# Moving the fourth cell of the head, and subtracting its sums on TensorE, in a fused mLSTM and gated MLP kernel

## The chip, the cores and the metric

The kernel runs on one core of one Trainium2 chip. The metric is the device time of one launch in microseconds (us). The engines are named as in the profile: PE is TensorE, with PEld for its loads of stationary operands; DVE is VectorE; ACT is ScalarE; POOL is GpSimd; SP issues most of the DMAs.

## The reference

Two blocks run one after the other. The first is an mLSTM cell over 4 batches, 8 heads, 768 steps and 40 dimensions a head:

```python
for t in range(S):
    m_new = np.maximum(f_gate[:, :, t] + m, i_gate[:, :, t])
    f_stab = np.exp(f_gate[:, :, t] + m - m_new)
    i_stab = np.exp(i_gate[:, :, t] - m_new)
    C = f_stab * C + i_stab * outer(vt, kt)
    n = f_stab * n + i_stab * kt
    y[:, :, t] = sigmoid(o_gate) * (C @ qt) / np.maximum(np.abs(n . qt), 1.0)
```

(The last lines are shortened.) The second takes the result as x, 3072 rows of 320, and computes `h = x @ w_in` (320 x 2048), `g = h * np.cos(h)`, `g @ w_out` (2048 x 320). The weights w_in and w_out come in 64-bit floats, which the kernel turns into 32-bit floats itself.

## The kernel before

The steps are cut into 6 chunks of 128. A cell n is one batch of one chunk: n = 4 * chunk + batch, 24 cells in all. Within a chunk the recurrence is written as products: with a running sum of the forget gates and a running maximum, cell n has a matrix E of decays, one 128x128 block for each of 8 heads. The scores of keys and queries (`scores`) are multiplied by E (`weigh`), and the products of that with the values (`values`) give the cell's output, which `normalize` divides by its denominator and multiplies by the sigmoid of the o gate. `seam` turns the output, so that it can be the input of the second block, and makes the increment of the carried state; `seam_out` and `state` copy both out of PSUM.

The first four cells (chunk 0) are the head of the kernel, `first_cells`. After it comes `first_period`, where the second block of chunk 0 begins beside cell 4 (`B` is 4); from there on both blocks are interleaved to the end. The order of the instructions on each engine is the order of the calls in the program, written by hand: no scheduler moves them. Each engine takes its own instructions in that order and waits where one is not ready, and so does the queue of SP for its DMAs.

For a cell of the head, `maxima_in` makes on PE, in PSUM, the running maxima of all its heads, spread over the partitions, with a wall of 1e30 above the diagonal. It is a product of the identity with `wall` and four products of `of_parts` columns (ones that pick a row) with `M0_parts`, which holds the maxima as the sum of three bf16 parts. `less_sums` subtracts, on DVE and in two halves of 128x512, what `tab` holds for each row, the input gate less the running sum (`a0`, turned); `decay` takes the exponential of the negative on ACT.

The gates of the other five chunks are worked out beside the head, by the 32 rows of batch and head: `gates_sums` and `gates_maxima` are scans on DVE, `gates_less_sums` and `gates_shifts` small steps, and `gates_carry` makes the carried factors and writes them to DRAM as G_d; the maxima go to M_d. `gates_exp` takes exponentials of `a1` less the chunk's last maximum, `gates_turn` turns `a1` and these exponentials by PE transposes of 32x128, and `gates_turn_out` copies both into `tab`.

The weights of the second block come in pieces: `weights_in(0)` issues the DMAs of the first two pieces (4 DMAs of 128 KB each, line 163) and of a low piece (4 of 64 KB, line 217). For each piece, `take_apart` is two steps on ACT (lines 175 and 177), `bound` two and `join` one on DVE (lines 181, 182 and 191), and `round_up` one on POOL (line 196). `warm` issues products of zeros on PE, which nothing reads.

Lines that the text speaks of: 749 and 743 first products of the second block; 757 their rounding on ACT (`near`); 863 the down products; 576 values and 560 scores of the head; 566 `weigh`; 650 to 658 `normalize`; 692 to 701 `seam`; 712 `seam_out`; 1096 `warm`; 325 `gates_turn`; 332 a small product for the carried factors; 328 `gates_turn_out`; 476 `decay` of later cells; 436 loads of E from M_d.

Of the kernel before, what the change touches and what calls it, by code (L numbers as in the profile page):

```python
# [11 lines left out]
FP = mybir.dt.float32  # L12
# [17 lines left out]
def kernel(  # L30
# [20 lines left out]
    nc = tc.nc  # L51
# [36 lines left out]
    M0_parts = small[:, 704:768].bitcast(BF)  # L88
    of_parts = small[:, 768:784].bitcast(BF)
    nc.vector.memset(nil, 0.0)  # L90
    ident = const.tile([128, 128], FP, name="ident")
# [8 lines left out]
    nc.vector.memset(M0_parts, 0.0)  # L100
    nc.vector.memset(of_parts, 0.0)

    nc.gpsimd.memset(wall, 0.0)
# [66 lines left out]

    def take_apart(dst, bits):
        n = dst.shape[1]
        hi, lo = bits[:, 0:n, 1], bits[:, 0:n, 0].bitcast(U32)

        nc.scalar.activation(out=dst, in_=hi.bitcast(FP), func=AF.Abs)

        nc.scalar.activation(out=bits[:, 0:n, 0], in_=lo, func=AF.Copy, scale=2.0 ** -29)
# [62 lines left out]
    nM1 = gates.tile([BH, R], FP, name="nM1")  # L240
    dd = gates.tile([BH, R - 1, BH], FP, name="dd")

    def gates_constants():
# [23 lines left out]
    def maxima_in_parts():  # L267
# [8 lines left out]
        nc.scalar.copy(out=M0_parts[BH:2 * BH], in_=mid)  # L276

    def gates_first_out():
        pg = ps_o.tile([128, 2, BH], FP, name="pg", tag="o")
        for j, src in enumerate((a0, e0)):  # L280
            nc.tensor.transpose(pg[:, j], src, ident[0:BH, 0:BH])
        nc.vector.tensor_copy(out=tab[:, 0, 0:2], in_=pg)
# [3 lines left out]

    eW, eG = shift, keep

# [24 lines left out]

    def gates_exp():
        for c in range(R):
            nc.scalar.activation(out=eW[:, c], in_=a1[:, c], func=AF.Exp, bias=nM1[:, c:c + 1])

# [4 lines left out]

    def gates_turn(pg, j):
        for c in range(R):
            nc.tensor.transpose(pg[:, c, j], (a1, eW)[j][:, c], ident[0:BH, 0:BH])

    def gates_turn_out(pg):
        nc.scalar.copy(out=tab[:, 1:NC, 0:2], in_=pg)

# [139 lines left out]
    def decay(n, heads=range(H)):  # L469
        c, b = divmod(n, B)  # L470
        if n < B:
            nc.scalar.activation(out=Es[n], in_=Es[n], func=AF.Exp, scale=-1.0)
            return
        for h in heads:
            g = b * H + h
            nc.scalar.activation(out=Es[n][:, h], in_=Es[n][:, h], func=AF.Exp, scale=-1.0, bias=tab[:, c, 0, g:g + 1])  # L476
# [167 lines left out]

    def normalize(n):
        c, b = divmod(n, B)
        hs = heads_of[n]
# [4 lines left out]
        nc.vector.reciprocal(out=dn, in_=dn)  # L652
        y = p1.tile([128, 3 * C], FP, name="y", tag="yt")[:, 0:DM]
        t = yo.rearrange("q (h d) -> q h d", h=H)
        nc.vector.tensor_tensor(out=t, in0=sig[c][:, b], in1=hs[:, :, 0:D], op=OP.mult)
        for lo, hi, o in ((0, 32, y[:, 0:KL].rearrange("q (g a d) -> q a g d", g=2, a=HP)),
                          (32, D, y[:, KL:DM].rearrange("q (a g d) -> q a g d", g=2, a=HP))):
            nc.vector.tensor_tensor(out=o, in0=t[:, :, lo:hi].rearrange("q (a g) d -> q a g d", g=2),
                                    in1=dn.rearrange("q (a g) -> q a g", g=2).unsqueeze(3).to_broadcast([128, HP, 2, hi - lo]), op=OP.mult)
# [448 lines left out]
    def first_cells():  # L1108
# [41 lines left out]
        weigh(0)  # L1150
        sigmoid_next()
        sigmoid(0)
        exp_next()
        gates_sums()
        gates_less_sums()
# [5 lines left out]
        less_sums(2)  # L1161
        decay(2)
        values(1)
        normalize(0)
        normalize(1)
        maxima_in(3)
        less_sums(3)
        turn(2)
        turn_out(2, False)
        weigh_k(2)  # L1170
        seam(0)
        seam_out(0)
        scores(2)
        state(0)
        decay(3)
        weigh(2)
        seam(1)
        seam_out(1)
        weigh_k(3)
        gates_maxima()  # L1180
        gates_shifts()
        load_M(B)
        load_blocks(B)
        load(B, "kv")
        outs.append((0, weights_out(0)))
        turn(3)
        turn_out(3, False)
        values(2)
        normalize(2)
        state(1)  # L1190
        gates_carry()
        load_G_of(B)
        load_blocks(B + 1)
        pg = ps_a.tile([128, R, 2, BH], FP, name="pg", tag="a")
        gates_turn(pg, 0)
        scores(3)
        take_apart(*pieces[0])
        seam(2)
        weigh(3)
        bound(pieces[0][0])  # L1200
        seam_out(2)
        gates_exp()
        take_apart(*pieces[1])
        warm(2, psum_o())
        values(3)
        join(*pieces[0])
        round_up(*pieces.pop(0))
        state(2)
        more = weights_in(1)
        pieces.append(next(more))  # L1210
        normalize(3)
        warm(6, psum_o())
        gates_turn(pg, 1)
        bound(pieces[0][0])
# [4 lines left out]
        seam_out(3)  # L1219
        gates_turn_out(pg)  # L1220
        take_apart(*pieces[0])
# [12 lines left out]
        decay(B)  # L1234
        odd_constants()
        odd_values_of(B)
# [418 lines left out]
```

## Time and profile before

| | us |
|---|---|
| median of 3 runs | 504.28 (503.46 to 504.53) |
| the profiled execution | 503.72 |
| its span, from the first to the last instruction | 501.9 |
| PE busy | 495.1 (99%) |
| DVE busy | 420.6 (84%) |
| ACT busy | 332.5 (66%) |
| POOL busy | 300.0 (60%) |

The profile is of one execution, whose own time stands beside its span. A timeline row has the start, the length, the engine, the line, the operation, its output and inputs, the shape and how many instructions are merged; in brackets stands how long the engine had been idle, and what released it. Matmuls are pipelined, so the length of a group on PE reaches over the start of the next; the time from start to start is what a group costs in a full stream. An f32 matmul appears as two instructions, a transpose as one. The granted clock of PE is 1.00 through the whole span.

### The profile page before, as it was taken

How to read it: one execution, taken by the hardware profiler on the slowest of the kernel's cores; microseconds unless marked ns; L12 is line 12 of the kernel's file. 1: busy time of each engine (PE TensorE's matmuls, PEld its weight loads, DVE VectorE, ACT ScalarE, POOL GpSimd, SP SyncE). 2: the span in 40 equal slices, each digit the busy share in tenths (PEclk: the TensorE clock that was granted, in tenths of full speed). 3: DMA queues.
4: the chain of work that ended last, by engine and by line, in shares of the span. 5: the costliest groups of instructions: out<-in, count | busy, mean ns of one | idle time of the engine just before them, and what ended most of it. 6: DMA issues, size and time to landing. Idle time of an engine off the chain costs nothing.

```text
span 501.9 us, 11143 instructions
## 1 busy us (share of the span) xinstructions
PE 495.1 (99%) x4038; PEld 375.4 (75%) x4038; DVE 420.6 (84%) x842; ACT 332.5 (66%) x646; POOL 300.0 (60%) x394
## 2 busy tenths in 40 slices
PE   9999999999999999999999999999999999999997
PEld 6856656565667668887887888788788888787876
DVE  7899998999878878899889889889979866777565
ACT  6799997878564575765877846777847743443541
POOL 8254557666555576787558877657567446434340
PEclk9999999999999999999999999999999999999999
DMA  9989899997366346129446118628113000010001
GB/s 139 182 223 239 213 224 279 233 217 136 114 178 111 101 120 127 50 86 202 132 125 106 48 54 195 168 83 150 43 35 85 1 7 5 2 54 0 2 0 54
DMA packets 100663, 56.74 MB, mean 113 GB/s; under 512 B 63456, under 2 KB 93360, under 8 KB 100608
## 3 DMA queue, kind: packets, MB, share of 16 engines
q1 hardware_dynamic: 97408, 54.43, 46.8%
q10 hardware_dynamic: 2896, 1.23, 1.0%
q8 instruction: 32, 0.52, 0.5%
q0 software_dynamic: 304, 0.36, 0.3%
q14 instruction: 23, 0.19, 0.1%
HBM read 50.66 MB, written 4.10 MB: 109 GB/s over the span
## 4 chain that ended last, share of the span: by engine, by line
PE 85%; ACT 4%; DVE 3%; DMA 2%; SPq 2%; POOL 2%; issue 1%; DVEq 0%; ACTq 0%; POOLq 0%
PE acc L1014 24%; PE pup L817 17%; PE pup L749 9%; PE po L863 6%; PE pup L833 6%; PE late L1014 5%; PE ps L560 4%; PE pup L743 3%; PE vt L595 2%; PE vt L586 2%; PE pu L701 2%; PE ph L576 1%; DMA E<-M_d 1%; DMA vs<-in_v_dram 1%; DVE n L760 1%
## 5 line engine op out<-in xcount | busy, mean ns | idle before, releaser
L757 ACT ACTIVATE n<-pup 128x512 int32<-128x512 f32 x64 | 37.0, 593 | 84.2 <-DVE pup L842 58.4
L765 ACT ACTIVATE n<-n 128x512 f32<-128x512 f32 x96 | 57.7, 626 | 16.5 <-DVE n L760 12.5
L852 POOL TENSOR_TENSOR g<-g,n 128x512 f32<-128x512 f32 x31 | 39.6, 1278 | 47.5 <-ACT n L765 47.4
L749 PE MATMUL pup<-xT,w_in_sb 128*128 128x512 f32 x128 | 58.7, 601 | 0.3 <-ACT xT L712 0.2
L1014 PE MATMUL acc<-w_out_sb,g 128*128 128x160 f32 x320 | 58.7, 303 | 0.0
L760 DVE SCALAR_TENSOR_TENSOR n<-pup,n 128x512 f32<-128x512 f32 x64 | 43.1, 689 | 18.5 <-ACT n L757 15.9
L834 POOL TENSOR_TENSOR blocks<-blocks 128x256 f32<-128x256 f32 x32 | 25.1, 785 | 54.5 <-ACT blocks L826 54.5
L1014 PE MATMUL acc<-T,g 128*128 128x160 f32 x304 | 56.4, 301 | 0.0
L817 PE MATMUL pup<-xT,w_in_sb 128*128 128x256 f32 x192 | 53.5, 385 | 0.2
L476 ACT ACTIVATE E<-E,tab 128x128 f32<-128x128 f32 x160 | 50.1, 389 | 4.3 <-POOL E L462 4.1
L1014 PEld LDWEIGHTS acc<-w_out_sb,g 128*128 128x128 f32 x320 | 49.0, 190 | 4.7 <-issue 2.7
L769 DVE TENSOR_TENSOR g<-pup,n 128x512 f32<-128x512 f32 x64 | 42.7, 687 | 5.7 <-ACT n L765 4.8
L1014 PEld LDWEIGHTS acc<-T,g 128*128 128x128 f32 x304 | 46.5, 190 | 1.1 <-issue 0.4
L749 PEld LDWEIGHTS pup<-xT,w_in_sb 128*128 128x128 f32 x128 | 23.1, 189 | 30.7 <-issue 30.0
L825 ACT COPY blocks<-pup 128x512 f32<-128x512 f32 x32 | 18.6, 582 | 34.2 <-PE pup L817 33.8
L817 PEld LDWEIGHTS pup<-xT,w_in_sb 128*128 128x128 f32 x192 | 33.8, 189 | 9.6 <-ACT blocks L826 4.4
L817 PE MATMUL pup<-x_room,room 128*128 128x256 f32 x128 | 38.5, 382 | 0.0
L542 POOL TENSOR_TENSOR qG<-t,G 128x512 f32<-128x512 f32 x20 | 26.4, 1321 | 16.7 <-DVE t L538 16.7
L1014 PE MATMUL acc<-T,blocks 128*128 128x160 f32 x160 | 36.2, 308 | 0.2 <-POOL blocks L904 0.2
L863 PE MATMUL po<-w_out_sb,g 128*128 128x320 f32 x128 | 36.2, 436 | 0.1
L833 PE MATMUL pup<-xL,w_in_l 64*128 64x512 f32 x128 | 36.1, 641 | 0.0
L566 DVE TENSOR_TENSOR E<-ps,E 128x512 f32<-128x512 f32 x46 | 29.5, 682 | 5.8 <-PE ps L560 5.6
(227 smaller groups left out, 1210.7 us busy)
## 6 DMA issues: line engine op xcount, KB each, us to landing
E<-M_d SPq DMA_DIRECT2D x20, 512.0 KB, 6.0
qr<-in_q_dram SPq DMA_DIRECT2D x72, 80.0 KB, 2.6
kr<-in_k_dram SPq DMA_DIRECT2D x72, 80.0 KB, 2.2
bits<-in_moe_w_out_dram SPq DMA_DIRECT2D x8, 640.0 KB, 6.2
G<-G_d SPq DMA_DIRECT2D x18, 256.0 KB, 5.7
blocks<-in_moe_w_in_dram SPq DMA_DIRECT2D x32, 128.0 KB, 4.6
out_dram<-o_sb SPq DMA_DIRECT2D x23, 160.0 KB, 1.8
o<-in_o_gate_dram SPq DMA_DIRECT2D x40, 80.0 KB, 4.4
```

The costliest lines, as they stand in the source:

```text
L476: nc.scalar.activation(out=Es[n][:, h], in_=Es[n][:, h], func=AF.Exp, scale=-1.0, bias=tab[:, c, 0, g:g + 1])
L566: nc.vector.tensor_tensor(out=w, in0=pss[n][j], in1=w, op=OP.mult)
L749: nc.tensor.matmul(pu.rearrange("p (b t) -> p b t", b=B), w_in_sb[:, i, ts(2 * f2 + e, 128)], xT[c][:, i:NK * B:NK], start=(i == 0 and not ...
L757: nc.scalar.activation(out=self.n[e], in_=self.pu[e], func=AF.Copy, bias=0.25)
L760: nc.vector.scalar_tensor_tensor(out=self.n[e].bitcast(FP), in0=self.pu[e], scalar=0.25, in1=self.n[e], op0=OP.add, op1=OP.subtract)
L765: nc.scalar.activation(out=r, in_=r, func=AF.Sin, scale=TWO_PI_DOWN)
L769: nc.vector.tensor_tensor(out=g, in0=self.pu[e], in1=self.n[e].bitcast(FP), op=OP.mult)
L817: nc.tensor.matmul(bank[:, part].rearrange("p (b t) -> p b t", b=B // 2), w[:, f2], x, start=start, stop=stop, skip_group_check=True)
L833: nc.tensor.matmul(pu, w_in_l[r, f2], xL[c][r].rearrange("p b t -> p (b t)"), start=False, stop=True, skip_group_check=True)
L852: tt(out=self.g, in0=self.g, in1=self.n[e].bitcast(FP), op=OP.mult)
L863: nc.tensor.matmul(po[c][b], gs[c, f][:, ts(b, C)], w_out_sb[:, f], start=(f == 0), stop=(f == NF - 1))
L1014: nc.tensor.matmul(a, lhs, rhs, start=start, stop=stop)
```

## The change

Four things change, all in the head.

Cell 3 gets its exponents on PE alone. `sums_in_parts` splits the negative of `a0` into three bf16 parts (five steps on DVE, one on ACT), and `exponents_in(3)` adds, to the wall and the maxima, one more product a half, of `a0_parts` with columns of `of_parts`. `less_sums(3)` goes, and the exponential of cell 3 reads PSUM, in two instructions. These products stand ahead of `values(1)`.

The exponentials of the later gates are taken after the turn: `gates_exp` and the second `gates_turn` go; `gates_last` makes on DVE a diagonal `dM` of the last maxima, `gates_less_last` adds `a1` turned by the identity and ones times `dM` on PE, 10 products of 32x128 by 32x32, and `gates_turn_out` is a copy and an exponential.

The calls of the head are put in another order. The scan of the maxima stands before `normalize(1)`; cell 3 is turned before cell 1's `seam`; `take_apart` of the first piece is split, its first step before `seam_out(1)`, its second after it; `bound`, `join` and `round_up` of that piece, and `gates_last`, stand before cell 2's `normalize` on DVE, which is itself split around `weigh(3)`; `seam(2)` stands behind `values(3)`. On SP, cell 4's blocks, k and v come before its E. The four memsets of `odd_constants` go from the end of the head to before `gates_less_sums`.

The fillers between the last cells go from 2 and 6 to 2 and 2.

```diff
+    def sums_in_parts():
+        rest, mid = blocks[0:BH, 38], blocks[0:BH, 39].bitcast(BF)[:, 0:C]
+        hi = a0_parts[0:BH]
+        nc.vector.tensor_scalar(out=hi, in0=a0, scalar1=-1.0, scalar2=None, op0=OP.mult)
+        nc.vector.scalar_tensor_tensor(out=rest, in0=a0, scalar=-1.0, in1=hi, op0=OP.mult, op1=OP.subtract)
+        nc.vector.tensor_copy(out=mid, in_=rest)
+        nc.vector.tensor_tensor(out=rest, in0=rest, in1=mid, op=OP.subtract)
+        nc.vector.tensor_copy(out=a0_parts[2 * BH:3 * BH], in_=rest)
+        nc.scalar.copy(out=a0_parts[BH:2 * BH], in_=mid)
+
+    def exponents_in(n):
+        for i in range(2):
+            g = n * H + HP * i
+            wall_in(n, i, psum_o())
+            nc.tensor.matmul(pm[n, i], a0_parts, of_parts[:, g:g + HP].unsqueeze(2).to_broadcast([128, HP, C]),
+                             start=False, stop=False)
+            spread(n, i)
...
-    def gates_exp():
-        for c in range(R):
-            nc.scalar.activation(out=eW[:, c], in_=a1[:, c], func=AF.Exp, bias=nM1[:, c:c + 1])
+    def gates_last():
+        nc.vector.tensor_tensor(out=dM, in0=ident[0:BH, 0:BH].unsqueeze(1).to_broadcast([BH, R, BH]),
+                                in1=nM1.unsqueeze(2).to_broadcast([BH, R, BH]), op=OP.mult)
...
+    def gates_less_last(pw):
+        for c in range(R):
+            nc.tensor.matmul(pw[:, c], a1[:, c], ident[0:BH, 0:BH], start=(c == 0), stop=False)
+            nc.tensor.matmul(pw[:, c], one.to_broadcast([BH, 128]), dM[:, c], start=False, stop=(c == R - 1))
+
+    def gates_turn_out(pg, pw):
+        nc.scalar.copy(out=tab[:, 1:NC, 0], in_=pg)
+        nc.scalar.activation(out=tab[:, 1:NC, 1], in_=pw, func=AF.Exp)
...
+            E = Es[n]
+            for i in range(2):
+                nc.scalar.activation(out=E[:, ts(i, HP)], in_=pm[n, i], func=AF.Exp, scale=-1.0)
...
         decay(2)
+        exponents_in(B - 1)
         values(1)
         normalize(0)
+        gates_maxima()
+        gates_shifts()
         normalize(1)
-        maxima_in(3)
-        less_sums(3)
         turn(2)
         turn_out(2, False)
         weigh_k(2)
+        decay(3)
         seam(0)
+        load_blocks(B)
+        load(B, "kv")
+        load_M(B)
+        outs.append((0, weights_out(0)))
+        scores(2)
         seam_out(0)
-        scores(2)
-        state(0)
-        decay(3)
         weigh(2)
+        turn(3)
+        turn_out(3, False)
+        take_high(*pieces[0])
         seam(1)
         seam_out(1)
         weigh_k(3)
-        gates_maxima()
-        gates_shifts()
-        load_M(B)
-        load_blocks(B)
-        load(B, "kv")
-        outs.append((0, weights_out(0)))
-        turn(3)
-        turn_out(3, False)
-        values(2)
-        normalize(2)
+        take_low(*pieces[0])
+        state(0)
         state(1)
         gates_carry()
         load_G_of(B)
         load_blocks(B + 1)
-        pg = ps_a.tile([128, R, 2, BH], FP, name="pg", tag="a")
-        gates_turn(pg, 0)
-        scores(3)
-        take_apart(*pieces[0])
-        seam(2)
-        weigh(3)
+        values(2)
         bound(pieces[0][0])
-        seam_out(2)
-        gates_exp()
-        take_apart(*pieces[1])
-        warm(2, psum_o())
-        values(3)
         join(*pieces[0])
         round_up(*pieces.pop(0))
-        state(2)
+        scores(3)
+        pgs = ps_a.tile([128, 2, R, BH], FP, name="pg", tag="a")
+        gates_turn(pgs[:, 0])
+        gates_last()
+        gates_less_last(pgs[:, 1])
+        bank = psum_o()
+        warm(2, bank)
+        y = weighted(2)
+        weigh(3)
+        divided(2, y)
+        take_apart(*pieces[0])
+        values(3)
+        warm(2, bank)
         more = weights_in(1)
         pieces.append(next(more))
+        seam(2)
+        seam_out(2)
+        state(2)
         normalize(3)
-        warm(6, psum_o())
-        gates_turn(pg, 1)
         bound(pieces[0][0])
         put_together(*pieces.pop(0))
...
         decay_exponents(B)
         seam(3)
         seam_out(3)
-        gates_turn_out(pg)
+        gates_turn_out(pgs[:, 0], pgs[:, 1])
```

More of the change, by code (lines that the diff above doesn't have):

```diff
@@ L89 @@
     of_parts = small[:, 768:784].bitcast(BF)
+    a0_parts = small[:, 784:848].bitcast(BF)
     nc.vector.memset(nil, 0.0)
@@ L101 @@
     nc.vector.memset(of_parts, 0.0)
+    nc.vector.memset(a0_parts, 0.0)
     nc.gpsimd.memset(wall, 0.0)
@@ L171, in take_apart, with take_high, take_low @@
     def take_apart(dst, bits):
+        take_high(dst, bits)
+        take_low(dst, bits)
+    def take_high(dst, bits):
+        nc.scalar.activation(out=dst, in_=bits[:, 0:dst.shape[1], 1].bitcast(FP), func=AF.Abs)
+    def take_low(dst, bits):
         n = dst.shape[1]
-        hi, lo = bits[:, 0:n, 1], bits[:, 0:n, 0].bitcast(U32)
-        nc.scalar.activation(out=dst, in_=hi.bitcast(FP), func=AF.Abs)
+        lo = bits[:, 0:n, 0].bitcast(U32)
         nc.scalar.activation(out=bits[:, 0:n, 0], in_=lo, func=AF.Copy, scale=2.0 ** -29)
@@ L241 @@
     dd = gates.tile([BH, R - 1, BH], FP, name="dd")
+    dM = gates.tile([BH, R, BH], FP, name="dM")
     def gates_constants():
@@ L285 @@
     flat = [t.rearrange("r c s -> r (c s)") for t in (F1, M1, a1, keep, shift)]
-    eW, eG = shift, keep
+    eG = keep
     def gates_sums():
@@ L321, in gates_diagonal, with gates_turn @@
                                 in1=eG[:, 0:R - 1, last].to_broadcast([BH, R - 1, BH]), op=OP.mult)
-    def gates_turn(pg, j):
+    def gates_turn(pg):
         for c in range(R):
-            nc.tensor.transpose(pg[:, c, j], (a1, eW)[j][:, c], ident[0:BH, 0:BH])
-    def gates_turn_out(pg):
-        nc.scalar.copy(out=tab[:, 1:NC, 0:2], in_=pg)
+            nc.tensor.transpose(pg[:, c], a1[:, c], ident[0:BH, 0:BH])
+    def gates_less_last(pw):
[5 more added lines that the diff above has]
+        nc.scalar.activation(out=tab[:, 1:NC, 1], in_=pw, func=AF.Exp)
     def gates_spread():
@@ L470, in decay @@
         c, b = divmod(n, B)
+        if n < B - 1:
+            nc.scalar.activation(out=Es[n], in_=Es[n], func=AF.Exp, scale=-1.0)
+            return
         if n < B:
-            nc.scalar.activation(out=Es[n], in_=Es[n], func=AF.Exp, scale=-1.0)
+            E = Es[n]
+            for i in range(2):
+                nc.scalar.activation(out=E[:, ts(i, HP)], in_=pm[n, i], func=AF.Exp, scale=-1.0)
             return
@@ L645, in normalize, with weighted @@
     def normalize(n):
+        divided(n, weighted(n))
+    def weighted(n):
         c, b = divmod(n, B)
@@ L652, in normalize, with divided @@
         nc.vector.reciprocal(out=dn, in_=dn)
-        y = p1.tile([128, 3 * C], FP, name="y", tag="yt")[:, 0:DM]
         t = yo.rearrange("q (h d) -> q h d", h=H)
         nc.vector.tensor_tensor(out=t, in0=sig[c][:, b], in1=hs[:, :, 0:D], op=OP.mult)
+        return t, dn
+    def divided(n, of):
+        t, dn = of
+        y = p1.tile([128, 3 * C], FP, name="y", tag="yt")[:, 0:DM]
         for lo, hi, o in ((0, 32, y[:, 0:KL].rearrange("q (g a d) -> q a g d", g=2, a=HP)),
@@ L1151, in first_cells @@
         sigmoid_next()
+        gates_sums()
+        sums_in_parts()
         sigmoid(0)
         exp_next()
-        gates_sums()
+        odd_constants()
         gates_less_sums()
@@ L1234, in first_cells @@
         decay(B)
-        odd_constants()
         odd_values_of(B)
```

## The prediction

> **What bounds the kernel now.** The page's first part comes first: PE is busy for 99% of the span, and the chain that ended last (part 4) is 85% PE. From 55 us on I find PE without gaps that this change could touch, so the change is worth what it moves the start of that stretch. I therefore read the timelines of the first 60 us, engine by engine. TensorE, around the last two cells of the head:
>
> ```profile
> 22.04 1.88 PE L576 MATMUL ph<-vs,E 128*128 128x41 f32 x16
> 23.85 0.49 PE L325 MATMUL pg<-ident,w_out_sb 32*128 32x32 f32 x5
> 24.27 1.16 PE L560 MATMUL ps<-t,t 64*128 64x128 f32 x16
> ...
> 26.95 1.87 PE L576 MATMUL ph<-vs,blocks 128*128 128x41 f32 x16
> 28.65 1.47 PE L1096 MATMUL pm<-room 128*128 128x512 bf16 x6
> 30.05 0.49 PE L325 MATMUL pg<-ident,w_out_sb 32*128 32x32 f32 x5
> 30.54 0.41 PE L692 MATMUL px<-ident,y 128*128 128x128 f32 x2
> ```
>
> The columns are start, length, engine, line, operation. Groups follow start to start: PE looks full, but L1096 is filler, which means waiting. VectorE says for what:
>
> ```profile
> 25.54 1.29 DVE L566 TENSOR_TENSOR blocks<-ps,blocks 128x512 f32<-128x512 f32 x2
> 26.91 0.50 DVE L181 TENSOR_SCALAR w_in_sb<-w_in_sb 128x512 f32<-128x512 f32 x1
> ...
> 28.86 0.17 DVE L650 SCALAR_TENSOR_TENSOR dn<-ph,least 128x8 f32<-128x8 f32 x1 [0.18 <-PE ph L576]
> ```
>
> The chain is: scores of cell 3, end 25.43; their weighing (L566), end 26.83; values of cell 3, 26.95 to 28.65; its normalizing; its turned output at 30.54 (call this the pivot). From the start of cell 3's values to the pivot is 30.54-26.95 = 3.59 us, whatever PE does beside it. Behind the pivot ScalarE carries the path without a gap:
>
> ```profile
> 31.37 0.37 ACT L712 COPY xT<-px 128x256 f32<-128x256 f32 x1
> 31.64 0.43 ACT L328 COPY tab<-pg 128x320 f32<-128x320 f32 x1
> 31.95 0.45 ACT L175 ACTIVATE w_in_l<-blocks 128x256 f32<-128x256 f32 x1
> ...
> 34.82 2.45 ACT L476 ACTIVATE E<-E,tab 128x128 f32<-128x128 f32 x8
> 37.29 1.08 ACT L757 ACTIVATE n<-pup 128x512 int32<-128x512 f32 x2
> ```
>
> From 37.29 to 55.40 the busy time by stage is 17.66 of 18.11 us for ACT and 17.04 for DVE, so a delay of the first rounding (L757) passes through to the end.
>
> **Up to cell 2's values: nothing.** The changed program has the products of cell 3's maxima and sums ahead of cell 1's values. From 13.14 us (maxima of cell 2) on PE, start to start: maxima 0.88; cell 3's exponents, 0.88 like these plus two more 128x512 bf16 products at 0.22, 1.32; values 1.77; turn 0.88; turned output of cell 0 1.02; scores 1.09; turn 0.88; turned output of cell 1 1.02: 8.86, so cell 2's values start at 22.0, against 22.04. What is saved on order (0.2 of waiting for v) is paid by the two products. The five small DVE steps that make the parts cost what the same five cost at L271 to L275, 3.71 to 5.29, 1.58; they lie in a gap of 1.53 before cell 1's weighing: 0 to 0.1. DVE loses the subtraction of cell 3 (2 x 0.64), and ACT gets its exponential as two 128x512 from PSUM instead of one 128x1024: both are off the path here. POOL's four memsets (36.00 to 37.25, 1.25) now stand before the subtraction of the later gates (11.85); it then ends at 14.9, and its reader, the maxima scan, starts at 17.2: hidden; if that cover went, up to 1.25 for the scan. SP issues E's load after the next cell's blocks, k and v, near 28.0 instead of 26.70; with the 4.8 to 6.7 us that such loads took it lands by 34.7 at worst, before its mask (about 35): hidden, narrowly.
>
> **Where it hurts: the first piece of w_in.** ACT's first conversion of that piece now follows the turned copies of cell 3, which end near 21.7, and DVE's bounding and joining of it stand ahead of cell 3's weighing. Has the piece landed? SP's queue:
>
> ```profile
> 17.59 4.42 SPq L163 DMA_DIRECT2D blocks<-in_moe_w_in_dram  x8
> 22.37 2.71 SPq L217 DMA_DIRECT2D blocks<-in_moe_w_in_dram  x4
> ...
> DMA to landing us min/median/max: 4.0/4.1/4.2
> ```
>
> The first piece is the first four of the eight. The fourth is issued at 19.72, so it lands at about 19.72+4.1 = 23.8. Bounds: not before 22.35, when the first L217, which the built program makes wait for the landing of the first of the eight, went out; not after 24.5, when the last L217, which waits for the fourth, had started. Nothing ahead of these issues changes on SP. So ACT stands from 21.7 to 23.8, with cell 1's copies, its states and the carry queued behind it, and DVE, done with cell 2's weighing at 21.95, stands to 23.8+0.66 = 24.46. Then DVE: bound and join 1.77 (26.91 to 28.68 before), 26.2; the new product dM (32x160; L320's 32x128 took 0.27) 0.3, 26.5; the first half of cell 2's normalizing 0.99 (23.96 to 24.95), 27.5; cell 3's weighing 1.29, 28.8, where it ended at 26.83.
>
> **PE between.** Scores of cell 3 end at 24.9 (0.5 earlier: cell 1's output and the first turn of the gates are no longer in between), five transposes 0.42, 25.35. Then come ten new f32 matmuls, each two passes: a 32x128 stationary, 32 columns moving. They wait for dM at 26.5; 18 of 20 passes are left. The nearest rows for one pass:
>
> ```profile
> L576 PEld LDWEIGHTS ph<-vs,E 128*128 128x128 f32 x48 | 5.6, 192 | 0.3 <-DVE E L566 0.3
> L325 PEld LDWEIGHTS pg<-ident,w_out_sb 32*128 32x128 f32 x10 | 0.8, 136 | 0.5 <-ACT w_in_sb L175 0.4
> L332 PEld LDWEIGHTS pd<-dd,one 32*128 32x128 f32 x2 | 0.3, 182 | 0.1
> ```
>
> L325 has the same shape, but is a transpose: 136 ns a load and 0.42/5 = 0.084 from start to start. L332 is a true f32 matmul with 32 rows, and its load of 182 ns is near L576's 192, which runs at 1.71/16 = 0.107 a pass. I take 0.107: 18 x 0.107 = 1.93, 28.45 (with 0.084: 1.51, 28.0). [...] Two fillers 0.44: cell 3's values start at 28.9, against 26.95: **+1.95**. DVE's 28.8 would give nearly the same, so both would have to improve. Behind them the two fillers and cell 2's output fit in the 3.59 (1.70+0.44+1.02 = 3.16); four fillers and five transposes fewer there save nothing, for the normalizing ends last.
>
> **ACT behind the pivot.** One 128x320 copy becomes a 128x160 copy and a 128x160 exponential; the 128x128 forms took 0.25 and 0.30, so about 0.27+0.32 less 0.31 to 0.43: +0.15 to +0.3, taken as **+0.25**. The five 32x128 exponentials that go (1.57) had 0.13 us of waiting behind them, off the path.
>
> **Carry.** It moves from 24.74 to about 26.9 on ACT, so G lands some 2 us later and SP waits about 3 us for it; its readers are delayed by the same 2 us, and their slack stays: nothing.
>
> **Sum.** +1.95+0.25 = +2.2. The profiled execution took 503.72 (span 501.9 and 1.8 around it), which gives 505.9; the three runs' median lies 0.56 above it, which gives 506.5. I take the middle, **506.2**. With the landing at 22.4 the values start at 27.55 (+0.6, +0.85 in all), at 24.5 at 29.6 (+2.65, +2.9); the cheap pass takes up to 0.4 off.
>
> **Rivals.** (1) The piece is there when ACT asks, at 21.7. Then DVE bounds it in its gap, the weighing ends at 26.5, and PE decides alone: 25.35+20 x 0.107+0.44 = 27.9, +1.0 and 0.25: 505.4; at 0.084 a pass 504.9. Against it: the landing rows. For it: only that the order would then fit. It straddles the line of no change. (2) Not slower: the new products overlap, at the 0.0275 a pass of L701's 16 in 0.44 (its stationary has 40 columns), and the piece lands by 21.7. Then DVE's 26.5 decides the values' start, 0.45 before now; with 0.25 paid behind the pivot that is -0.2, 503.8. If the exponential hides, and L181 and L182 on the last piece of w_in (2.25 us at 32.44, while POOL is busy; 0.29 and 0.30 at 73.41) get free of POOL's mask, PE's idle 0.56 before L743 goes too: -1.0, 503.0. It needs passes under 0.05 and a landing before 22.0; no row with 128 columns shows that. (3) Clock: PE stands about 1.1 us for dM and 0.4 before the pivot. The granted clock was 1.00 in all stages, with an idle 0.56 at most in this stretch. If it were halved for the 3 us of work that follow, 1.5 to 3 more: 508. (4) The later G costs: SP's wait of 3 us reaches the second part of w_in, whose first conversion had 2 us of slack: 0 to +1 more, 507.
>
> [...]
>
> **Numbers.** Chances: forecast 0.70, (4) 0.06, (1) 0.14, (2) 0.07, (3) 0.03. A measurement here tells 0.2% (1.0 us) from no change. The forecast's case falls under +1.0 only with an early landing and the cheap pass (0.06 of its 0.70), (1) is half within, and of (2) I give 0.04 to its better end: slower 0.64+0.06+0.07+0.03 = 0.80, within 0.06+0.07+0.03 = 0.16, faster 0.04. The range 504.2 to 507.8 reaches from below (1) to the late landing with some of (4); (2), (3) and the ends of the others are left out.
>
> **What would show it.** In the changed kernel: ACT idle for about 2 us before its first conversion of w_in, released by a DMA; DVE idle from about 22 to 24.5; dM near 26.3; the ten products with a pass near 0.1; cell 3's values at 28.9, its turned output at 32.5 and the first rounding at 39.5, 2.2 late. Wrong if the conversion starts at 21.7, if the values start before 27.5, or if the roundings are late and the end is not.

## The result and the profile after

| | before | after |
|---|---|---|
| median, us | 504.4 (4 runs, 503.46 to 505.51) | 509.0 (4 runs, 508.88 to 510.38) |
| ratio, 95% interval | | 1.0096 (1.0070 to 1.0123) |
| profiled execution, its span | 503.72, 501.9 | 508.88, 507.0 |
| mean granted clock of PE | 1.0 | 0.993 |

The kernel is slower by 4.6 us, the profiled span by 5.1. The forecast was +2.2 and its range ended at 507.8. PE around the last two cells, for the changed kernel (values are L614 now, scores L598, seam L737 to L746, filler L1141; L475 begins cell 3's exponents; L356 and L357 are the ten products):

```profile
15.84 0.38 PE L475 MATMUL pm<-room 128*128 128x512 bf16 x1 [1.02 <-DVE E L604]
...
23.88 1.98 PE L614 MATMUL ph<-vs,E 128*128 128x41 f32 x16
...
27.21 0.38 PE L356 MATMUL pg<-ident,w_out_sb 32*128 32x32 f32 x2
...
29.98 3.04 PE L614 MATMUL ph<-vs,blocks 128*128 128x41 f32 x16
...
33.66 0.63 PE L737 MATMUL px<-ident,y 128*128 128x128 f32 x2
...
35.49 0.69 PE L737 MATMUL px<-ident,y 128*128 128x128 f32 x2
```

Cell 3's values start at 29.98 (before 26.95), and they take 3.04 us where cell 2's same sixteen take 1.98. The pivot, cell 3's turned output, stands at 35.49 (before 30.54). The windows of that stretch say why; the columns are the stretch, its length, busy time of PE, PEld, DVE, ACT and POOL with counts, then the granted clock, the DMA share and GB/s:

```profile
29.00:30.00 1.00, 1.00 (x9) 0.81 (x9) 0.36 (x2) 1.00 (x2) 0.76 (x2) 1.00 1.19 215
30.00:31.00 1.00, 1.00 (x9) 1.00 (x7) 0.00 (x0) 0.05 (x1) 0.98 (x2) 0.72 1.05 248
33.00:34.00 1.00, 1.00 (x5) 0.45 (x2) 0.88 (x4) 0.00 (x0) 0.00 (x0) 0.50 1.02 388
37.00:38.00 1.00, 1.00 (x14) 0.68 (x11) 0.35 (x3) 1.00 (x5) 0.81 (x1) 0.87 0.15 53
```

PE's clock falls to half at 30.44 and is back at 37.27 by the trace's record of it, 6.83 us, with PE busy for all of every microsecond. In the profile before, the record has no fall while the kernel works; it begins with the clock's first rise, at 4.16 us, ahead of which nine 512-column fillers stood 0.43 us apart instead of 0.22. VectorE, and GpSimd's subtraction of the later gates:

```profile
13.42 1.56 POOL L320 TENSOR_TENSOR w_out_sb<-w_out_sb 32x640 f32<-32x640 f32 x1
13.61 1.45 DVE L293 CAST room<-blocks 32x128 bf16<-32x128 f32 x1
...
24.99 0.43 DVE L187 TENSOR_SCALAR w_in_sb<-w_in_sb 128x512 f32<-128x512 f32 x1 [1.58 <-ACT w_in_sb L178]
...
26.52 0.31 DVE L342 TENSOR_TENSOR dM<-ident,nM 32x160 f32<-32x160 f32 x1
...
27.61 1.28 DVE L604 TENSOR_TENSOR blocks<-ps,blocks 128x512 f32<-128x512 f32 x2
...
33.05 0.17 DVE L691 SCALAR_TENSOR_TENSOR dn<-ph,least 128x8 f32<-128x8 f32 x1 [3.70 <-PE ph L614]
```

The last of the five steps that make the parts (L293) took 1.45 us; the same cast took 0.22 at L275 of the kernel before and at L282 of this one. DVE then waits for the first piece of w_in, and after the weighing of cell 3 it stands idle for 3.70 us, waiting for PE: the work between is PE's now. Behind the pivot, on ScalarE, nothing is lost that the pivot had not lost already:

```profile
24.28 0.67 ACT L178 ACTIVATE w_in_sb<-blocks 128x512 f32<-128x512 f32 x1 [0.54 <-DMA blocks<-in_moe_w_in_dram]
...
36.85 0.37 ACT L757 COPY xT<-px 128x256 f32<-128x256 f32 x1 [0.50 <-PE px L739]
...
40.37 2.45 ACT L514 ACTIVATE E<-E,tab 128x128 f32<-128x128 f32 x8
42.84 1.08 ACT L802 ACTIVATE n<-pup 128x512 int32<-128x512 f32 x2
```

The first rounding (L802) starts at 42.84, 5.55 later than before; the end is 5.1 later.

### The profile page after: what moved, and what is told of

Its sections match the earlier page's. It is cut to its first block, busy times and chain, and to the rows that moved or that the text cites. A ratio compares the mean times of both kernels' runs of the same rounds, so it can differ in the third digit from the quotient of the medians.

```text
span 507.0 us, 11167 instructions
## 1 busy us (share of the span) xinstructions
PE 500.0 (99%) x4051; PEld 380.5 (75%) x4051; DVE 420.3 (83%) x847; ACT 331.6 (65%) x644; POOL 300.5 (59%) x394
## 4 chain that ended last, share of the span: by engine, by line
PE 88%; DVE 3%; ACT 3%; issue 1%; POOL 1%; SPq 1%; DMA 1%; DVEq 0%; ACTq 0%; POOLq 0%
PE acc L1059 25%; PE pup L862 18%; PE pup L794 9%; PE pup L878 6%; PE po L908 6%; PE late L1059 4%; PE ps L598 4%; PE pup L788 3%; PE vt L633 2%; PE vt L624 2%; PE pu L746 2%; PE ph L614 1%; DMA G<-G_d 1%; DVE n L805 1%; PE pw L1141 1%
## 5 line engine op out<-in xcount | busy, mean ns | idle before, releaser
L802 ACT ACTIVATE n<-pup 128x512 int32<-128x512 f32 x64 | 37.0, 593 | 84.7 <-DVE pup L887 58.5
L887 DVE TENSOR_TENSOR pup<-pup,blocks 128x256 f32<-128x256 f32 x32 | 13.9, 434 | 24.2 <-PE pup L878 23.9
## 6 DMA issues: line engine op xcount, KB each, us to landing
E<-M_d SPq DMA_DIRECT2D x20, 512.0 KB, 6.2
```

Source lines behind the costliest of these rows:

```text
L802: nc.scalar.activation(out=self.n[e], in_=self.pu[e], func=AF.Copy, bias=0.25)
```

## The experiments

Each run's result lists the mean granted clock. One stretch of 3.41 us at half clock lowers it by 0.0034 over 505 us, so the number of such stretches can be read for every run, not for the profiled one alone: 1.000 or 0.999 is none, 0.997 or 0.996 one, 0.993 two, 0.990 three, 0.987 four (a fall behind the last work takes up to 0.001 more). The mean tells how many stretches there are, not where they lie; the place is recorded for the profiled run alone. Beside the experiments the kernel before had one in 13 of its 103 runs, and those took 506.2 to 507.0; the other 90 took 503.2 to 505.6.

**First round: the kernel after with one part changed.** I first held that the ten products alone bring the clock down, and that a filler before each pair would hold it. That is dense_fill:

```diff
         for c in range(R):
+            warm(1, bank)
             nc.tensor.matmul(pw[:, c], a1[:, c], ident[0:BH, 0:BH], start=(c == 0), stop=False)
```

> The changed kernel with one filler (a 128x512 bf16 product of zeros) ahead of each of the five pairs of small products. Theory A (PE's clock falls because a stretch of small products, 32 rows by 32 columns, counts as little work although PE is never idle): the clock stays at 1.00 from the first microseconds on; PE has 5 x 0.22 = 1.1 us more to do, and the stretch at half clock goes (1.1 on cell 3's values, about 1.3 on the two turned outputs): 507.4 to 508.0 against 509.0. Rival B (the clock falls for another reason, PE's stand at 15 us or the fewer fillers behind cell 3's values): it still falls, 1.1 us more: 510.1.

511.0 (510.26 to 512.65), ratio 1.0127 (1.0095 to 1.0158). The clock fell for two or three stretches in all four runs: five fillers are not enough, and they cost 2 us by the medians. The second takes the products out: ScalarE makes the exponentials again and PE turns them ahead of cell 3's seam.

```diff
-            nc.tensor.matmul(pw[:, c], a1[:, c], ident[0:BH, 0:BH], start=(c == 0), stop=False)
-            nc.tensor.matmul(pw[:, c], one.to_broadcast([BH, 128]), dM[:, c], start=False, stop=(c == R - 1))
+            nc.tensor.transpose(pw[:, c], shift[:, c], ident[0:BH, 0:BH])
...
-        gates_last()
-        gates_less_last(pgs[:, 1])
...
         divided(2, y)
+        gates_exp()
         take_apart(*pieces[0])
...
         normalize(3)
+        gates_less_last(pgs[:, 1])
```

> The changed kernel with its ten small products and dM undone: exponentials on ACT and a second turn by transposes, ahead of cell 3's turned output; the rest as changed, fillers 2 and 2. Theory A: the clock holds, PE has 2.2 us less ahead of cell 3's values and no half clock behind them: 504.5 to 505.5. Rival B: only the 2.2 go, the clock still falls: 506.8. Rival C (the late first piece of w_in sets the path by DVE): the weighing of cell 3 still ends near 28.7, values start at 28.8 instead of 29.98: about -1.2 without the clock's share, -3.6 with it.

507.31 (505.46 to 508.78, 10 runs), ratio 1.0062 (1.0043 to 1.0081). Without the products six of ten runs show no half-clock stretch, one shows one, two two, one three; so the clock also falls without them, in four runs of ten (the kernel before: 13 of 103), and with them it fell in all four runs of the kernel after. About 3 us stay even where it holds (505.5 to 508.5, against 504.07), which neither the products nor the clock explains; theory A gave 504.5 to 505.5.

The cast of 1.45 us stood beside GpSimd's subtraction of the later gates. sums_first makes the parts ahead of the scan (`sums_in_parts()` before `gates_sums()`), odd_back puts GpSimd's four memsets back to the end of the head.

> The changed kernel with the five DVE steps that make the parts of the sums ahead of the scan of the forget gates. Theory D (the last of the five, a cast of 32x128 that took 1.45 us instead of 0.22, stood because POOL was subtracting at the same time): the cast takes 0.25, PE's idle 1.0 us at 15 us shrinks to about 0.2; 508.2, the clock falls as before. Rival: the scan itself, now behind, holds cell 1's weighing as long: no change, 509.0.

> The changed kernel with POOL's four memsets back at the end of the head. If the memsets put POOL's subtraction onto the cast, the cast is free again and PE's idle 1.0 goes: 508.0. If any subtraction beside the five steps stops them, it now meets an earlier one of the five and the stand is about as long: 508.5 to 509.0. POOL's masks and copies at the end of the head have slack: the move back costs nothing there.

509.97 (507.74 to 510.6), ratio 1.0096 (1.0065 to 1.0126), and 508.9 (508.64 to 509.8), ratio 1.0084 (1.0058 to 1.0109). Neither took the stand away: in the first, the 32x128 multiplication took 1.32 us beside GpSimd's weighing of k and memsets; in the second a multiplication took 1.38 and a subtraction 1.54. In each run the step that stood was one that met GpSimd's work. Both kept the fall of the clock.

**Second round: halves of the change.** sums_alone is the kernel before with cell 3's sums by products, order_alone the kernel after without them, seam_back the kernel after with cell 2's normalizing and seam ahead of cell 3's values as before, products_as_fill the kernel before with

```diff
-        gates_exp()
+        gates_last()
...
-        warm(6, psum_o())
-        gates_turn(pg, 1)
+        gates_less_last(pgs[:, 1])
```

> The first half of the change by itself: the kernel before, with cell 3's sums subtracted by products, their three parts made by VectorE behind the scan of the gates, the products ahead of cell 1's values, cell 3's exponent read from PSUM. The order of cells 2 and 3, their fill and the second gate table stay as before. Theory T (TensorE's clock is halved when a stretch of about 3.4 us holds mostly thin passes, as the turns, the ten products and cell 3's values are; no idle is needed for it): no thin stretch is added, so the clock stays at 1.0 from its first rise on, and the cost is what VectorE's long cast beside GpSimd takes, weighing(1) later and TensorE idle for 0.5 to 1.7 us near 15 us: 504.6 to 505.8. Rival I (the clock falls because TensorE stood idle near 15 us): the same idle is there, so the clock is at 0.5 for 6.8 us somewhere between 24 and 38 us, and the time is 506.5 to 508.

> The second half by itself: the kernel after, but cell 3's sums are added and subtracted as before (maxima_in(3) and less_sums(3) behind cell 1's normalizing), so VectorE makes no parts near 13 us. Theory T: the thin stretch (turns, ten products, cell 3's values) is there, so the clock is at 0.5 for 6.8 us from about 28 to 32 us on, and the time is 507.3 to 508.6 (509.0 less about 1.0 of idle near 15 us, with two subtractions of VectorE back near 20 us). Rival I: no idle near 15 us, so the clock holds and the time is 505.5 to 506.5, the ten products (2.2 us) alone.

> The kernel after with cell 2's seam (its eight 64-row and four or more 128-column passes) back between cell 3's scores and cell 3's values, right behind the ten products, cell 2's whole normalizing ahead of it on VectorE, and six fillers behind cell 3's values in the seam's old place. Theory T: seam and fillers stand on both sides of the thin passes; the clock holds or falls for one stretch of 3.4 us only; with the clock held 506.4 to 507.6 (after 509.0, less 2.5 for the clock, plus up to 0.8 as the seam stands ahead of cell 3's values again). If the clock falls all the same for 6.8 us: 509 to 511, and the seam's place has nothing to do with it.

> The kernel before with one edit: ScalarE's five exponentials of the gates leave, and the six fillers and five second turns behind cell 3's values are replaced by the ten products, of 32 rows each, in that same place, where TensorE waits for cell 3's normalizing anyway; one exponential reads them from PSUM at the end. Theory T: ten thin passes right behind cell 3's values, thin too, make a thin stretch of over 3.4 us, so the clock falls to 0.5 near 31 to 35 us for 3.4 or 6.8 us, and the time is 505.0 to 506.5. Rival P (the products cost only where they stand ahead of cell 3's values; the clock fell in the kernel after for another reason): the clock holds and the time is 503.6 to 504.5.

| | median | ratio, 95% interval | stretches at half clock |
|---|---|---|---|
| sums_alone | 506.0 | 1.0033 (1.0019 to 1.0048) | none in 10 runs |
| order_alone | 509.76 | 1.0103 (1.0066 to 1.0141) | two: 508.69, 509.05; three: 510.48, 510.67 |
| seam_back | 513.25 | 1.0167 (1.0120 to 1.0214) | two: 512.0, 512.3; four: 514.2, 514.5 |
| products_as_fill | 506.01 | 1.0029 (1.0005 to 1.0053) | one: 504.8 to 505.5 (5 runs); two: 506.5 to 508.2 (5 runs) |

Rival I falls for a stand of this length: sums_alone has PE idle for 1.09 us near 15 us, and its clock holds. seam_back misses theory T's 506.4 to 507.6 by 6 us: with cell 2's whole normalizing ahead, dM came later, PE stood for 1.7 us between 27 and 29, and the clock fell further; so the seam's place alone does not hold it, and more can't be read from that run. products_as_fill is theory T's best support so far: one edit in the kernel before, the clock falls in every run. But it removes fillers and adds products at once.

order_alone also shows what the first half is worth inside the whole: nothing that four runs can tell. Without it the kernel takes, at two stretches, 508.69 and 509.05, where the kernel after takes 508.88 and 508.99. Its VectorE and TensorE:

```profile
25.23 0.43 DVE L187 TENSOR_SCALAR w_in_sb<-w_in_sb 128x512 f32<-128x512 f32 x1 [2.27 <-ACT w_in_sb L178]
...
27.12 0.40 PE L357 MATMUL pg<-dM,one 32*128 32x32 f32 x2 [0.67 <-DVE dM L342]
```

PE reaches the products at 26.07 here, but waits for dM until 27.12, because bounding stands for 2.27 us for the piece of w_in. In the kernel after, PE comes 1.14 later (0.50 of it stood already at cell 2's maxima, 13.77 against 13.27), finds dM there, and the row stands at 27.43. All but 0.3 us of what the first half loses lies inside the wait for that piece.

**Third round: fillers and products apart, and the rest.** fill_and_products is products_as_fill with the six fillers kept; no_fill is the kernel before with `warm(6, psum_o())` deleted; late_piece is no_products with `bound`, `join` and `round_up` of the first piece behind `divided(2, y)`; all_three is late_piece with cell 3's sums as before too.

> The kernel before with the ten products in place of the five second turns of the gates behind cell 3's values, and its six 512-column fillers kept ahead of them (products_as_fill had left the fillers out). The thin passes are the same as in products_as_fill, whose clock fell to 0.5 for 3.4 or 6.8 us in all ten runs. Theory T (the clock falls for want of dense passes in a stretch of about 3.4 us): with the fillers' 1.3 us back between thin passes, the clock holds at 1.0 in at least half of the runs (mean granted clock 0.999 to 1.0), and the time is 503.6 to 505.0. Rival Q (the products themselves bring the clock down, whatever stands beside them): mean clock 0.993 to 0.997 in every run, 505 to 507.5.

> The kernel before without the six fillers behind cell 3's values, and nothing else changed: no products, the second gate table turned as before. TensorE stands idle there instead, for about 1.3 us. Theory T: cell 3's values (41-column passes) and the idle leave a thin stretch of over 3.4 us, so the clock falls in most runs, mean clock 0.993 to 0.997, and the time is 505 to 507. Rival Q (it is the products): no product here, so the clock is 0.999 to 1.0 in as many runs as in the kernel before (28 of 33), and the time is 503.5 to 504.2.

> The kernel no_products (the kernel after, with ScalarE's five exponentials and five second turns in place of the ten products) with VectorE's bound, join and GpSimd's rounding of the first piece of w_in moved behind cell 2's division, so that nothing ahead of cell 3's weighing waits for that piece. Theory L (the piece's late landing holds cell 3's weighing, and its landing differs from run to run, which is why no_products took 505.5 to 508.8 even where its clock held): weighing(3) ends near 27 us instead of 28.3, cell 3's values start 1 us earlier, and runs whose clock holds agree within 1 us, at 505.0 to 506.3. Rival: TensorE's order decides there, the time stays at 506.7 to 508.

> The kernel late_piece with cell 3's sums added and subtracted as before as well: of the change only the order is left (cell 3's scores ahead of the gates' turns, four fillers, cell 2's seam behind cell 3's values, the moved transfers and memsets). The three costs that I name (VectorE's parts beside GpSimd's work, the ten products, the first piece's wait ahead of weighing(3)) are all taken away. If they are the whole of it: 503.5 to 504.8 with a clock that holds. If the clock falls without the products (cell 3's values with two fillers on each side make a thin stretch): 505.5 to 507, mean clock 0.993 to 0.997. If the seam's place behind cell 3's values costs by itself: 505 to 506 with the clock at 1.0.

| | median | ratio, 95% interval | stretches at half clock |
|---|---|---|---|
| fill_and_products | 506.56 | 1.0042 (1.0019 to 1.0065) | none: 505.5 to 505.9 (4 runs); one: 506.4 to 508.9 (6) |
| no_fill | 504.53 | 1.0021 (0.9996 to 1.0045) | none: 503.3, 503.8; one: 504.2 to 504.7 (4); two: 505.4 to 508.2 (4) |
| late_piece | 507.5 | 1.0059 (1.0032 to 1.0087) | none in 7 runs |
| all_three | 507.48 | 1.0061 (1.0042 to 1.0080) | none: 506.5, 507.8; one: 505.7 to 509.2 (8) |

no_fill has half-clock stretches in eight of ten runs without a product. In its profiled run (two stretches) the second, 34.82 to 38.23, stands behind the place of the deleted fillers: rival Q falls, and by the counts (eight of ten runs with a fall without the six fillers, 13 of 103 with them) the fillers, which nothing reads, earn their place by holding the clock. The first, 17.75 to 21.16, stands ahead of that place, behind 1.53 us in which PE waited for v from the DMA. The one stretch of fill_and_products' profiled run, 17.54 to 20.95, lies there too, behind a wait for v of 1.31 us, and its ten products, from 32.99 on, ran at the full clock. So in both the clock also fell behind a stand of PE, of 1.53 and 1.31 us, and the counts of these two runs may mix both places. In time both missed: fill_and_products took 505.5 to 505.9 where its clock held, not 503.6 to 505.0, and no_fill's median lies below its 505 to 507. late_piece is a miss: its clock held, cell 3's weighing no longer waited for the piece, and it still took 505.4 to 508.5. GpSimd and VectorE in its timeline show that I had moved the cost:

```profile
30.45 1.31 POOL L202 TENSOR_TENSOR w_in_sb<-w_in_sb,blocks 128x512 int32<-128x512 int32 x1
30.55 1.65 DVE L702 TENSOR_TENSOR y<-room,dn 128x256 f32<-128x256 f32 x2
```

GpSimd's rounding of the piece now stood beside the division of cell 3's output, whose two steps took 1.65 us instead of 0.56, and the pivot stood at 32.11. all_three has the same collision (1.87 us) and settles nothing on the order by itself.

**Fourth round: the same time, thick and thin.** dense_ten and thin_ten add 2.2 us of PE at one place of the kernel before, ahead of cell 3's values, and nothing else:

```diff
-        warm(2, psum_o())
+        warm(12, psum_o())
         values(3)
```

is dense_ten, and thin_ten is

```diff
-        warm(2, psum_o())
+        bank = psum_o()
+        warm(2, bank)
+        for _ in range(10):
+            nc.tensor.matmul(bank[:, 0, 0:BH], one.to_broadcast([BH, 128]), ident[0:BH, 0:BH], start=True, stop=True)
         values(3)
```

> The kernel before with ten fillers more (512 columns each, 0.22 us apart, so 2.2 us of TensorE) ahead of cell 3's values, behind its two. Theory T: the clock holds (0.999 to 1.0 in as many runs as in the kernel before, about 5 of 6), and the time is that of 2.2 us of TensorE ahead of cell 3's values alone: 505.3 to 506.3. Rival S (any TensorE time put there costs what the kernel after lost, the clock's fall being a by-product): 508 to 509.5.

> The same place and the same TensorE time as in dense_ten, but as ten products of 32 rows and 32 columns (two passes each, 0.11 us a pass) whose result nothing reads. Theory T: the clock falls to 0.5 for one to three stretches of 3.41 us in all runs, mean clock 0.990 to 0.997, and the time is 506.8 to 508.8, that is 1.5 to 2.5 above dense_ten. Rival S: the two agree within 0.5 us. If the clock falls in both or in neither, theory T falls.

dense_ten took 505.67 (505.27 to 508.64, 10 runs), ratio 1.0029 (1.0006 to 1.0051); nine runs have no stretch at half clock, one has one. thin_ten took 509.63 (507.31 to 511.63, 6 runs), ratio 1.0106 (1.0074 to 1.0138), with one to three stretches in every run. PE's timeline in dense_ten, and a window of it:

```profile
26.91 2.76 PE L1096 MATMUL pm<-room 128*128 128x512 bf16 x12
29.51 1.87 PE L576 MATMUL ph<-vs,blocks 128*128 128x41 f32 x16
```

```profile
30.00:34.00 4.00, 4.00 (x46) 2.89 (x45) 2.40 (x9) 1.71 (x7) 0.51 (x1) 1.00 1.10 234
```

and the same of thin_ten:

```profile
27.41 2.41 PE L1207 MATMUL pm<-ident,one 32*128 32x32 f32 x20
29.75 3.13 PE L576 MATMUL ph<-vs,blocks 128*128 128x41 f32 x16
```

```profile
30.00:34.00 4.00, 4.00 (x20) 3.16 (x20) 0.98 (x5) 1.55 (x6) 0.47 (x1) 0.54 1.11 234
```

Cell 3's values start within 0.24 us of each other, 29.51 and 29.75, and PE is busy for the whole window in both; one runs at 1.00, the other at 0.54. The difference of the medians, 509.63-505.67 = 4.0 us, is the price of the passes being thin. This settles that the clock can fall for thin passes with PE never idle: in thin_ten it was busy for 4.00 us of 4.00 from 26 to 30 us too, ahead of the fall. The two kinds of pass differ in rows, columns and type at once (fillers are bf16, these products f32), which no run takes apart. The other two ask how much thinness matters: five of the ten products become one of 160 columns,

```diff
+        nc.tensor.matmul(pw.rearrange("p c r -> p (c r)"), one.to_broadcast([BH, 128]), dM.rearrange("q c r -> q (c r)"),
+                         start=True, stop=False)
         for c in range(R):
-            nc.tensor.matmul(pw[:, c], a1[:, c], ident[0:BH, 0:BH], start=(c == 0), stop=False)
-            nc.tensor.matmul(pw[:, c], one.to_broadcast([BH, 128]), dM[:, c], start=False, stop=(c == R - 1))
+            nc.tensor.matmul(pw[:, c], a1[:, c], ident[0:BH, 0:BH], start=False, stop=(c == R - 1))
```

once in the kernel after (one_wide) and once in fill_and_products (wide_fill).

> The kernel after with the five products of the ones with the diagonal maxima made one of 160 columns ahead of the other five: twelve passes instead of twenty, about 0.8 us of TensorE less ahead of cell 3's values. Theory T: the stretch is still thin (turns, ten narrow passes, cell 3's values), so the clock falls for one or two stretches, and the time is 507.3 to 508.5, the 0.8 us and perhaps a stretch. If the narrow products alone do it, the clock holds in half of the runs and those take 505.5 to 506.5.

> The kernel fill_and_products (the kernel before, its five second turns replaced by products behind the six fillers, ScalarE's five exponentials gone) with the products in one of 160 columns and five of 32: about 1.35 us behind the fillers instead of 2.2. fill_and_products took 505.5 to 505.9 where its clock held, 1.8 above the kernel before, and its TensorE decided the start of cell 3's seam. Theory T: TensorE is 0.8 us shorter there, so 504.6 to 505.2 where the clock holds, still above the kernel before by the rest of the products' time. If ScalarE's freed 1.6 us are worth something, 503.3 to 504.0, faster than before.

one_wide: 508.5 (505.33 to 509.82), ratio 1.0070 (1.0040 to 1.0101); at one stretch 507.0, at two 507.8 to 508.6, at three 509.8. Its two runs without a stretch took 505.33 and 509.21, and I can't account for the second. wide_fill: 504.99 (504.71 to 508.02), ratio 1.0033 (1.0008 to 1.0058); six runs without a stretch at 504.7 to 505.0, four with one at 507.5 to 508.0. Fewer passes help, as expected, by 0.8 us against fill_and_products; ScalarE's freed time buys nothing.

**Fifth round: what the first half costs by itself.** sums_alone had an accident: ScalarE's copy of the middle part came behind a sigmoid and two table loads, so PE waited 0.69 us more. sums_clean issues scan and parts ahead of the sigmoid; parts_late makes the parts behind `less_sums(2)` and the products behind `values(1)`.

> sums_alone with the scan of the gates and the three parts issued ahead of the first cell's sigmoid, as in the kernel after, so that ScalarE's copy of the middle part doesn't stand behind the sigmoid and two table loads (0.69 us of TensorE's idle in sums_alone). Theory V (VectorE's operations on 32x128 stand while GpSimd's subtraction of 32x640 runs, 1.2 us lost, weighing(1) that much later, and nothing behind it gives it back): 504.7 to 505.5 with the clock held. Rival: the stand is absorbed before cell 2's values, 503.7 to 504.3.

> The same products, with the three parts made behind cell 2's subtractions on VectorE (near 16 us, where GpSimd has no operation) and the products behind cell 1's values. Theory V: each of the five steps takes 0.15 to 0.3 us, 1.2 in all, which takes the place of cell 3's two subtractions (1.28) on VectorE, and the time is that of the kernel before: 503.5 to 504.3. Rival W (the products for cell 3, 1.5 us of TensorE ahead of cell 2's turns, cost by themselves): 504.7 to 505.5, the same as sums_clean.

sums_clean took 505.06 (504.47 to 506.18, 10 runs), ratio 1.0019 (1.0001 to 1.0036), against 503.70: +1.4 with the clock held in all ten. GpSimd and VectorE in its timeline:

```profile
12.20 1.53 POOL L315 TENSOR_TENSOR w_out_sb<-w_out_sb 32x640 f32<-32x640 f32 x1 [0.39 <-DVE w_out_sb L312]
...
12.28 1.60 DVE L285 SCALAR_TENSOR_TENSOR blocks<-blocks,room 32x128 f32<-32x128 f32 x1
```

The step that takes 0.28 elsewhere ends at 13.88, 0.15 behind GpSimd's. parts_late took 505.43 (504.71 to 506.8), ratio 1.0036 (1.0020 to 1.0051). Its five steps took 0.20 to 0.28 us each, as expected, but that gained nothing: PE then waited 1.01 us for the parts themselves. So the stand is shown, and so is the price of the first half, but not that the stand alone makes it: the other place has a wait of its own.

No version was faster than the kernel before; the nearest that keep a part of the change are wide_fill and sums_clean, at +1.1 and +1.4 of median.

## Why the prediction was wrong

- **"Up to cell 2's values: nothing" failed.** They start at 23.88, not 22.0. The five steps took 2.57 (12.49 to 15.06), not 1.58, so the gap of 1.53 did not hold them, and PE stood 1.02 us for cell 1's weighing. POOL's memsets were called hidden since their reader was far away; what I had not counted is VectorE's stand beside POOL's subtraction, 1.45 us for a cast that took 0.22 elsewhere. By itself it is +1.4 (sums_clean). In the whole it cost nothing that order_alone's runs can tell, for the wait for the piece covers most of it. Some of the 1.84 is that run's own: its clock first rose at 6.55 us, before at 4.16, and the maxima of cell 2 already start 0.63 later.
- **"Where it hurts: the first piece of w_in" was right.** ScalarE's conversion at 24.28 (forecast 23.8), dM done at 26.83 (26.5), the weighing's end at 28.89 (28.8). But ScalarE waited 0.54 us for the piece, not two: cell 3's turned copies ended at 23.75, not at 21.7.
- **"PE between" was right in its rate.** From 27.21 to 29.54, 2.33 us for 20 passes and their end, 0.112 a pass in the pairs; forecast 0.107. The loads beside them:

```profile
L356 PEld LDWEIGHTS pg<-ident,w_out_sb 32*128 32x128 f32 x10 | 1.5, 190 | 0.0
```

  190 ns, as for the 128-row loads and not the transposes' 136. Values at 29.98 instead of 28.9: +3.03, not +1.95. In this trace PE decided: it came to the products at 27.21, 0.38 behind dM, with all twenty passes to do instead of eighteen. That the first point's delay made this is not shown: order_alone, without the first half, waited for dM until 27.12, and its values started at 30.06, with the two fillers ahead of them already at half clock (0.82 us instead of 0.44). dense_ten gives 2.2 us at that place a price of +1.8 by medians (505.67 against 503.87), near the forecast's term.
- **The step that failed is the 3.59 us from cell 3's values to the pivot, "whatever PE does beside it", with "four fillers and five transposes fewer there save nothing".** From cell 3's values to the pivot it took 35.49-29.98 = 5.51. The filler was priced as PE's waiting and so at nothing; what it did was to keep the clock (without the six of them, no_fill's clock fell in eight of ten runs). In its half clock the sixteen values took 2.83 start to start (1.70 before), and seam and fillers stood behind them. At full clock the pivot would come the old 1.89 us behind the values' end, at 29.98+1.70+1.89 = 33.57, so 1.92 of its lateness is the clock's; the seam after it, from 35.49 to 36.85, gives another 0.53. That estimate of 2.45 from one trace lies below the 4.0 that thin_ten and dense_ten give, where three stretches fell in the profile. Without the 2.45 the first rounding would be 3.1 late instead of 5.55, with 0.63 of it that run's start: 2.5, against the forecast's 2.2. That the terms of the 2.2 are each right does not follow: no_products, without the products and with its clock held, still took about 3 us more than the kernel before, and why stays open.
- **Rival 3 was the one, at a chance of 0.03, and for a reason that it did not name.** It asked for PE to stand; by its busy time PE did not stand ahead of the fall (3.00 us busy of 3.00 from 27 to 30). I had taken the little idle time before, 0.56 us at most, as cover.
- **"ACT behind the pivot, +0.25": +0.07.** From xT to the first decay 40.37-36.85 = 3.52, before 3.45.
- **"Passes through to the end" was right:** 5.55 at the rounding, 5.1 at the end. In 18 of the 20 profiled runs, before and after among them, 464.1 to 464.6 us lie between the first rounding and the end of the span.
- **Rivals 1, 2 and 4:** the piece was not there early, no pass was cheap, and nothing behind the pivot grew by more than 0.1 beyond the seam at half clock, so a later G cost nothing to be seen.

## What to carry to other kernels

Price a filler by what the clock would do without it, not by the time it fills: where PE's passes were thin (32 rows by 32 columns), a busy PE was no cover here, and the same 2.2 us cost 1.8 us as 512-column passes and 5.8 as 32-column ones. Read the granted clock of every run, since its fall changed from run to run: 13 of 103 runs of the kernel before had it too. Before a small VectorE step is put into a gap, look at what GpSimd does in that gap (a cast of 0.22 us took 1.45), and before work is shortened ahead of a wait, ask what else ends there: two delays here covered each other.

## What the runs showed of the hardware

- The granted clock fell behind 3.41 us in which PE was busy all the time in the kernel after, dense_fill, odd_back, products_as_fill and thin_ten; in the other profiled runs with a fall PE also stood in that time, for 0.3 to 1.5 us. The falls lasted 3.41 (no_fill, from 34.82), 6.83 (the kernel after), 10.24 (thin_ten) and 13.65 us (seam_back), that is 1 to 4 times 3.413, and came a whole number of such stretches after the first rise: 6.55 to 30.44 is seven times 3.413, and so is 6.42 to 30.31 in products_as_fill.
- A count from the rows of the traces, made afterwards and tested by no run: for each pass that starts in a stretch of 3.413 us take its moving columns (twice for f32, whose 512-column pass took 0.44 us against 0.22 for bf16), times the rows and the columns of its stationary operand, each as a share of 128. The kernel after has 1786 and 2182 in the two stretches from 27.03 us, thin_ten 1242, 2438 and 2700 from 26.92, no_fill 1312 in the stretch with its wait for v, and half clock followed each of them. dense_ten has 5326 and 5762 from 27.60, the kernel before 4710 and 5066 from 24.64, and the full clock followed. What of the work the clock goes by is not shown: these stretches differ in shapes, types and waits at once.
- In all 20 profiled runs PE began with the same fillers at 0.99 us, but the first rise came at 3.71 to 6.55 us, and with it the place of the stretches. That may be why one kernel has runs with none, one and two of them; it is not shown, as each kernel has one profiled run.
- A VectorE operation of 32x128 on SBUF took 1.45 us in the kernel after, 1.60 in sums_clean, 1.61 in sums_alone and 1.54 in odd_back, instead of 0.22 to 0.28, while a GpSimd subtraction of 1.53 to 1.56 us ran that had begun before it, and ended within 0.15 us behind it; in late_piece two steps of 128x256 took 1.65 us instead of 0.56 beside GpSimd's rounding of 1.31.
- Open: late_piece ran from 505.4 to 508.5 with a clock that held, so something other than the clock varies there; the collision with GpSimd's rounding is seen in its one profile, and that it varies from run to run was not shown. Of the 2.7 us that this profile's span is longer than before, 1.65 stand ahead of the first rounding and 1.1 behind it.
